# Pooled attention and two feed-forward blocks on one core: the sums of v and the first w1/w2 conversions placed later in the fold

## The chip, the core and the metric

The kernel runs on one core of a Trainium2 chip. The core has TensorE (PE in the profile: matrix products and transposes, results in PSUM), VectorE (DVE), ScalarE (ACT), GpSimd (POOL) and SyncE (SP); the last two mainly issue DMA transfers here. Each engine works off its own instruction queue; engines wait for one another through semaphores. The metric is the device time of one execution in microseconds (us).

## What is computed

The reference, cut to its core:

```python
k_p = k.reshape(B, H, Sp, 8, D).mean(axis=3)      # B=8, H=8, S=576, D=64, Sp=72
v_p = v.reshape(B, H, Sp, 8, D).mean(axis=3)
attn = softmax(q @ k_p.T / sqrt(D))
x = (attn @ v_p).transpose(0, 2, 1, 3).reshape(4608, 512)
x = ((x @ w1) * (x @ w2)) @ w3 @ w_out            # 512 -> 1024 -> 1024 -> 512
xn = x / rms(x) * rms_g
out = (silu(xn @ w_gate) * (xn @ w_val)) @ w_out2 # 512 -> 1536 -> 512
```

## The kernel before

**The fold.** The product of w3 and w_out does not depend on the tokens, so the kernel computes it first (loop `for n in range(NW3)`, 16 tiles of w3). Weights arrive as 64-bit words of which a conversion makes float32. For each w3 tile that takes, in this order: a load on SP (L127), L144 and L147 on ScalarE, L165 and L174 on VectorE, and L177 on VectorE, which writes the tile `f`. TensorE transposes `f` (`tr_w3`, L576) into a PSUM tile, ScalarE copies that out as `hl` (L578), and TensorE makes four products with it (L681), summing in four PSUM banks `wps`. After eight tiles the sums are split into a high and a low part (L100 on ScalarE, L101 on VectorE: `wph`, `wpl`) and stored to DRAM from POOL (L700, L701).

**The attention of batch 0 and the first conversions of w1 and w2 run inside the fold.** They stand in a list `aux` of small steps, which a `Ticker` deals out after the products from the 31st on. `att_steps.flat()` gives the steps of the attention: for each of five query tiles (128 tokens, the last 64) the scores of four heads at a time (`step_S`: L338 on TensorE, the maximum L350 on VectorE, four exponentials L353 on ScalarE), the transposes of q (`step_Q`, L320, L325), the norm (`step_N`: L364, L365, L366 on VectorE), and the transposes of the tile before (`step_T`: L388, copied out by L393). `step_v` adds up pairs of rows of v (L260, L264 on VectorE; the other halvings were done by an accumulating DMA); `av_steps` then multiplies with v (L441) and writes the attention output as a high and a low part (L448 on ScalarE, L449 on VectorE).

The list `side` holds ten steps: `w_tiles` (which allocates), six steps that convert the first four pieces of w1, and three that begin on w2. A w1 or w2 piece takes L144 on ScalarE, L153, L165, L174 and L177 on VectorE, then a split into a high part (L100) and a low part (L101). `side` is spread evenly over `aux` from place `half` on.

**What sets the order.** The program is written as a sequence of steps, and a scheduling layer turns it into one queue per engine; it may move instructions within limits, except those marked `keep_in_program_order` (L144, L165, the first sum of v L260, and the pinned conversions among them). The order on each engine is fixed when the program is built.

**Buffers that tie loads to steps.** The pool `raw` has three buffers. Through them go, in turn, the two halves of batch 0's k, the left half of its v (`kv_369`), then the four pieces of w2 (`raw_469`, `raw_471`, `raw_473`, `raw_475`), then batch 1's k (`kv_881`, `kv_884`) and the left half of its v (`kv_887`). So `raw_473` is loaded when `kv_369` has been summed, and `kv_884` when `raw_473` has been converted. Each half of k or v is loaded in two transfers: a plain one from SP (L254) and an adding one from POOL (L255) when the first has landed.

After the fold the kernel multiplies the attention output of token block 0 with w1 and w2 (`ab`, lines 104 to 106), and from there attention of the next batch runs between these products. The time after 131 us is that of the token blocks and of the second feed-forward block.

Of the kernel before, what the change touches and what calls it, by code (L numbers as in the profile page):

```python
# [21 lines left out]
def kernel(  # L22
# [248 lines left out]
    def att_steps(b):  # L271
# [36 lines left out]
        def step_Q(g, hf):  # L308
            if 2 * g >= NTL:
                return  # L310
            tiles = TILES[2 * g : 2 * g + 2]
            nu, n = len(tiles), tiles[0][1]
            qt = q_t[g].rearrange("s u h d -> s u (h d)")
            if hf == 0:
                qT_t[g] = at_p.tile([P, 2, NP, P], F32, tag="qT", name="qT", bufs=2)
            qT = qT_t[g]
            if hf < nu:
                ps = apsum()
                for p in range(NP):
                    nc.tensor.transpose(  # L320
                        ps[:, p * P : p * P + n],
                        qt[:n, hf, p * P : (p + 1) * P],
                        ident[:n, :n],
                    )
                nc.scalar.copy(  # L325
                    qT[:, hf, :, :n], ps.rearrange("d (p s) -> d p s", p=NP)[:, :, :n]
                )
            if hf == 1:
                q_t.pop(g)
                load_q(g + 2)  # L330

        def step_S(t, hf):
            s0, n = TILES[t]
            ps = apsum()
            if hf == 0:
                s_t[t] = sbuf[t % len(sbuf)]
            for p in (2 * hf, 2 * hf + 1):
                nc.tensor.matmul(  # L338
                    ps[:n, (p % 2) * 2 * SP : (p % 2 + 1) * 2 * SP],
                    qT_t[t // 2][:, t % 2, p, :n],  # L340
                    kT[:, p, :],
                    start=True,
                    stop=True,
                )
            pv = ps[:n, : 4 * SP].rearrange("t (h s) -> t h s", s=SP)
            if hf == 0:
                mx_t[t] = at_p.tile([P, H, 1], F32, tag="mx", name="mx", bufs=2)
                den_t[t] = at_p.tile([P, H, 1], F32, tag="den", name="den", bufs=2)
            mx = mx_t[t][:n, 4 * hf : 4 * hf + 4, :]
            nc.vector.tensor_reduce(out=mx, in_=pv, axis=AX.X, op=ALU.max, negate=True)  # L350
            for j in range(4):
                h = 4 * hf + j
                nc.scalar.activation(  # L353
                    s_t[t][:n, h, :SP],
                    pv[:, j, :],
                    AF.Exp,
                    bias=mx[:, j, :],
                    accum_out=den_t[t][:n, h, :],
                )

        def step_N(t):
            s0, n = TILES[t]
            den = den_t.pop(t)
            nc.vector.tensor_scalar_add(den[:n], den[:n], 1e-9)  # L364
            nc.vector.reciprocal(out=den[:n], in_=den[:n])  # L365
            nc.vector.tensor_tensor(  # L366
                out=s_t[t][:n, :, :SP],
                in0=s_t[t][:n, :, :SP],
                in1=den[:n].to_broadcast([n, H, SP]),
                op=ALU.mult,  # L370
            )

        def step_T(t, hf):
            s0, n = TILES[t]
            if t == 0 and hf == 0:
                st8["aT", b] = at_p.tile([SPP, H, S], F32, tag="aT", name="aT")
            aT = st8["aT", b]
            if b >= 2:
                for i in range(2 * hf, min(2 * hf + 2, n // 32)):
                    for kb in range(SPP // 32):  # L380
                        nc.vector.transpose(  # L381
                            aT[32 * kb : 32 * kb + 32, :, s0 + 32 * i : s0 + 32 * i + 32],
                            s_t[t][32 * i : 32 * i + 32, :, 32 * kb : 32 * kb + 32],
                        )
                return
            ps = apsum()
            for j in range(4):
                nc.tensor.transpose(  # L388
                    ps[:SP, j * P : j * P + n], s_t[t][:n, 4 * hf + j, :SP], ident[:n, :n]
                )  # L390
            src = ps[:SP].rearrange("s (h t) -> s h t", h=4)[:, :, :n]
            dst = aT[:SP, 4 * hf : 4 * hf + 4, s0 : s0 + n]
            nc.scalar.copy(dst, src)  # L393
# [11 lines left out]
        def flat():  # L405
            steps = [step_kT, lambda: step_Q(0, 0), lambda: step_Q(0, 1)]
            for t in range(NTL):

                def d(t=t):
                    if t > 0:  # L410
                        step_T(t - 1, 0)
                    step_N(t)

                def e(t=t):
                    if t > 0:
                        step_T(t - 1, 1)

                steps += [
                    lambda t=t: step_S(t, 0),
                    lambda t=t: step_Q(t // 2 + 1, t % 2),  # L420
                    lambda t=t: step_S(t, 1),
                    d,
                    e,
                ]
            steps[20:20] = [step_v]
            return steps

        return SimpleNamespace(
            flat=flat, k0=step_k0, k1=step_k1, q=load_q, kT=step_kT, Q=step_Q,
            S=step_S, N=step_N, T=step_T, load_v=load_v, v=step_v,  # L430
        )
# [26 lines left out]
    def av_steps(b, i):  # L458
        return [lambda p=p: av_step(b, i, p) for p in range(NP)]
# [191 lines left out]
    aux[8:8] = [s0(*js[4:])]  # L651
    aux += [s0(*j1), lambda: A.T(NTL - 1, 0), lambda: A.T(NTL - 1, 1)]
    aux += av_steps(0, 0)
    half = 11
    side = [w_tiles] + c0[0] + c0[1][:3]
    for n, st in enumerate(side):
        aux.insert(half + (len(aux) - half) * n // len(side), st)
# [273 lines left out]
    half = [pos[2 * n] + pos[2 * n + 1] for n in range(KF1)]  # L931
# [649 lines left out]
```

## Time and profile before

| what | value |
|---|---|
| three runs | 1597.33, 1599.2, 1599.76 us (median 1599.2) |
| the profiled execution | 1597.47 us |
| its span, first to last instruction | 1595.4 us |
| TensorE busy | 1575.3 us (99%) |
| VectorE busy | 1101.3 us (69%) |
| ScalarE busy | 722.3 us (45%) |

A row of the timeline gives the start in us from the span's start, the length, engine, line, operation, written tile <- read tiles, shapes and count; in brackets how long the engine had been idle before, and what ended that. Lengths of neighbours overlap: what an operation costs in a full queue is the distance from its start to the next. A product of two float32 matrices is two or more instructions in the trace, so a row "x4" of L681 is two products. Busy times of TensorE are modelled, so a busy TensorE can still be slower than it might be.

### The profile page before, as it was taken

How to read it: one execution, taken by the hardware profiler on the slowest of the kernel's cores; microseconds unless marked ns; L12 is line 12 of the kernel's file. 1: busy time of each engine (PE TensorE's matmuls, PEld its weight loads, DVE VectorE, ACT ScalarE, POOL GpSimd, SP SyncE). 2: the span in 40 equal slices, each digit the busy share in tenths (PEclk: the TensorE clock that was granted, in tenths of full speed). 3: DMA queues.
4: the chain of work that ended last, by engine and by line, in shares of the span. 5: the costliest groups of instructions: out<-in, count | busy, mean ns of one | idle time of the engine just before them, and what ended most of it. 6: DMA issues, size and time to landing. Idle time of an engine off the chain costs nothing.

```text
span 1595.4 us, 22251 instructions
## 1 busy us (share of the span) xinstructions
PE 1575.3 (99%) x8114; PEld 1297.4 (81%) x8114; DVE 1101.3 (69%) x1945; ACT 722.3 (45%) x1692; POOL 81.4 (5%) x70
## 2 busy tenths in 40 slices
PE   7999999999999999999999999999999999999999
PEld 3567877877877888888888898898898899899888
DVE  7787789978985357789443447686469647775556
ACT  6867444444442245576422434344424433534422
POOL 0011100110000000014000000000000000000000
PEclk9999999999999999999999999999999999999999
DMA  9986644654461268888977666687666866676663
GB/s 281 314 247 128 149 140 125 160 131 132 108 241 47 93 260 325 315 321 298 322 244 244 211 188 195 196 256 227 192 198 200 286 188 191 198 241 185 190 187 97
DMA packets 197262, 328.96 MB, mean 206 GB/s; under 512 B 53657, under 2 KB 100761, under 8 KB 191522
## 3 DMA queue, kind: packets, MB, share of 16 engines
q1 hardware_dynamic: 182338, 305.48, 60.1%
q0 software_dynamic: 14816, 22.07, 6.2%
q8 instruction: 64, 1.05, 0.3%
q14 instruction: 44, 0.36, 0.1%
HBM read 250.89 MB, written 76.58 MB: 205 GB/s over the span
## 4 chain that ended last, share of the span: by engine, by line
PE 85%; DVE 9%; DMA 3%; ACT 1%; issue 1%; SPq 0%; DVEq 0%; POOLq 0%
PE ps L104 20%; PE ps L106 20%; PE ps L105 20%; PE y L106 4%; PE y L105 4%; PE y L104 4%; DVE aT L381 4%; PE o L104 2%; PE o L105 2%; PE o L106 2%; DMA raws<-in_moe_w_out_dram 2%; PE pa L441 2%; PE pa L338 2%; DMA kv<-in_k_dram 1%; PE wps L681 1%
## 5 line engine op out<-in xcount | busy, mean ns | idle before, releaser
L104 PE MATMUL ps<-xf,wr 128*128 128x512 f32 x576 | 225.1, 394 | 0.1
L105 PE MATMUL ps<-xf,wr 128*128 128x512 f32 x576 | 224.5, 390 | 0.0
L106 PE MATMUL ps<-xf,wr 128*128 128x512 f32 x576 | 224.4, 390 | 0.0
L1144 DVE TENSOR_TENSOR f<-y,f 128x512 f32<-128x512 f32 x48 | 33.1, 689 | 167.9 <-PE y L106 157.1
L381 DVE STREAM_TRANSPOSE aT<-s 32x256 f32<-32x256 f32 x324 | 140.8, 435 | 5.2
L1264 ACT COPY f<-ps 128x512 f32<-128x512 f32 x144 | 84.3, 586 | 128.3 <-PE ps L106 127.1
L104 PEld LDWEIGHTS ps<-xf,wr 128*128 128x128 f32 x576 | 108.1, 188 | 27.0 <-DVE f L1144 5.3
L106 PEld LDWEIGHTS ps<-xf,wr 128*128 128x128 f32 x576 | 108.1, 188 | 22.9
L105 PEld LDWEIGHTS ps<-xf,wr 128*128 128x128 f32 x576 | 108.2, 188 | 21.1
L353 ACT ACTIVATE s<-pa,mx 128x72 f32<-128x72 f32 (+1 forms) x280 | 85.6, 337 | 81.5 <-DVE mx L350 81.4
L104 PE MATMUL ps<-xh,w1h 128*128 128x512 f32 x288 | 117.6, 408 | 0.0
L106 PE MATMUL ps<-xh,w1l 128*128 128x512 f32 x288 | 112.8, 392 | 0.0
L105 PE MATMUL ps<-xl,w1h 128*128 128x512 f32 x288 | 112.8, 392 | 0.0
L104 PE MATMUL ps<-xh,w2h 128*128 128x512 f32 x288 | 112.6, 391 | 0.0
L106 PE MATMUL ps<-xh,w2l 128*128 128x512 f32 x288 | 112.3, 390 | 0.0
L105 PE MATMUL ps<-xl,w2h 128*128 128x512 f32 x288 | 112.2, 390 | 0.0
L590 ACT COPY f<-ps 128x512 f32<-128x512 f32 x70 | 41.6, 602 | 77.0 <-PE ps L106 73.2
L1144 DVE TENSOR_TENSOR f<-ps,f 128x512 f32<-128x512 f32 x96 | 65.0, 687 | 15.4 <-ACT hh L1274 8.2
L1144 DVE TENSOR_TENSOR acc<-ps,acc 128x512 f32<-128x512 f32 (+1 forms) x80 | 49.0, 633 | 33.8 <-PE ps L106 33.5
L104 PEld LDWEIGHTS ps<-xh,w1h 128*128 128x128 f32 x288 | 54.1, 188 | 17.4 <-issue 4.2
L105 PE MATMUL ps<-o,hf 128*128 128x256 f32 x240 | 67.9, 283 | 0.0
L106 PE MATMUL ps<-o,hf 128*128 128x256 f32 x240 | 67.9, 283 | 0.0
(250 smaller groups left out, 3917.5 us busy)
## 6 DMA issues: line engine op xcount, KB each, us to landing
wr<-wd SPq DMA_DIRECT2D x168, 512.0 KB
o<-od SPq DMA_DIRECT2D x96, 512.0 KB
hr<-hd SPq DMA_DIRECT2D x32, 512.0 KB
wd<-wst SPq DMA_DIRECT2D x16, 1024.0 KB
od<-ost SPq DMA_DIRECT2D x12, 1024.0 KB
wr<-wd SPq DMA_DIRECT2D x48, 256.0 KB
hd<-hh SPq DMA_DIRECT2D x33, 256.0 KB
q<-in_q_dram SPq DMA_DIRECT2D x32, 256.0 KB
```

The costliest lines, as they stand in the source:

```text
L104: nc.tensor.matmul(o, lh, rh, start=first, stop=False, skip_group_check=part)
L105: nc.tensor.matmul(o, lh, rl, start=False, stop=False, skip_group_check=part)
L106: nc.tensor.matmul(o, ll, rh, start=False, stop=last, skip_group_check=part)
L338: nc.tensor.matmul(ps[:n, (p % 2) * 2 * SP : (p % 2 + 1) * 2 * SP], qT_t[t // 2][:, t % 2, p, :n], kT[:, p, :], start=True, stop=True,)
L353: nc.scalar.activation(s_t[t][:n, h, :SP], pv[:, j, :], AF.Exp, bias=mx[:, j, :], accum_out=den_t[t][:n, h, :],)
L381: nc.vector.transpose(aT[32 * kb : 32 * kb + 32, :, s0 + 32 * i : s0 + 32 * i + 32], s_t[t][32 * i : 32 * i + 32, :, 32 * kb : 32 * kb + 32],)
L441: nc.tensor.matmul(ps[j * D : (j + 1) * D, :n], st8["vp", b][:, h * D : (h + 1) * D], st8["aT", b][:SP, h, c0 : c0 + n], start=True, stop= ...
L590: nc.scalar.copy(a0[i, m], ps)
L681: nc.tensor.matmul(wps[i], wt[:, i * P : (i + 1) * P], wo[j // 4][:, j % 4, :], start=j == 0, stop=j == KF1 - 1,)
L1144: nc.vector.tensor_tensor(out=out, in0=in0, in1=in1, op=op)
L1264: nc.scalar.copy(t, bank)
```

## The change

Two numbers: `step_v`, the sums of v, is put at place 27 of `flat()` instead of 20, which is behind the scores and the norm of the last query tile; and `half`, from where the ten steps of `side` are spread over `aux`, is 15 instead of 11. Nothing is added or removed.

```diff
-            steps[20:20] = [step_v]
+            steps[27:27] = [step_v]
...
-    half = 11
+    half = 15
     side = [w_tiles] + c0[0] + c0[1][:3]
     for n, st in enumerate(side):
         aux.insert(half + (len(aux) - half) * n // len(side), st)
```

VectorE, from the norm of the third query tile (L366, tile `s0_120`) to the L177 of the w3 tile that TensorE transposes next. Before (`f_581` is the w3 tile, the others are w1 pieces):

```order
L366 TENSOR_TENSOR s0_120<-s0_120,den_567 128x8x72
L153 TENSOR_SCALAR f_622<-raws_134 128x512
L165 SCALAR_TENSOR_TENSOR raws_137<-raws_137 128x512
L101 TENSOR_TENSOR w1l_503<-f_550,w1h_502 128x512
L177 ISA f_588<-raws_137,f_588 128x1024
L350 TENSOR_REDUCE mx_640<-ps_637 128x4
L165 SCALAR_TENSOR_TENSOR raws_134<-raws_134 128x512
L174 TENSOR_SCALAR f_622<-f_622 128x512
L177 ISA f_581<-raws_134,f_581 128x1024
```

After, the last twelve rows of that stretch (`f_583` is the w3 tile); between the norm and them stand six more, L153, L165, L153, L177, L165 and L174:

```order
L350 TENSOR_REDUCE mx_632<-ps_629 128x4
L177 ISA f_590<-raws_136,f_590 128x1024
L101 TENSOR_TENSOR w1l_542<-f_564,w1h_541 128x512
L153 TENSOR_SCALAR f_639<-raws_134 128x512
L165 SCALAR_TENSOR_TENSOR raws_137<-raws_137 128x512
L174 TENSOR_SCALAR f_613<-f_613 128x512
L101 TENSOR_TENSOR w1l_542<-f_590,w1h_541 128x512
L177 ISA f_613<-raws_137,f_613 128x1024
L165 SCALAR_TENSOR_TENSOR raws_134<-raws_134 128x512
L174 TENSOR_SCALAR f_583<-f_583 128x512
L174 TENSOR_SCALAR f_639<-f_639 128x512
L177 ISA f_583<-raws_134,f_583 128x1024
```

The w3 conversion stood eighth behind the norm and now stands eighteenth, with the w1 conversions (L101: their last step) ahead of it.

VectorE, the sums of v (L260, L264). Before, from the fourth w1 piece's L177 to the w3 tile `f_647`, which stands two rows further on:

```order
L177 ISA f_622<-raws_134,f_622 128x1024
L260 TENSOR_TENSOR kv_369<-kv_369 72x4x128
L350 TENSOR_REDUCE mx_640<-ps_673 128x4
L264 TENSOR_TENSOR vp_667<-kv_369 72x256
L260 TENSOR_TENSOR kv_372<-kv_372 72x4x128
L101 TENSOR_TENSOR w1l_503<-f_622,w1h_502 128x512
L264 TENSOR_TENSOR vp_667<-kv_372 72x256
L364 TENSOR_SCALAR den_641<-den_641 128x8
L174 TENSOR_SCALAR f_647<-f_647 128x512
L365 RECIPROCAL den_641<-den_641 128x8
L174 TENSOR_SCALAR f_693<-f_693 128x512
L366 TENSOR_TENSOR s1_121<-s1_121,den_641 128x8x72
```

After, from the norm of the last query tile on (`f_702` is the last w3 tile, `raw_469` and `raw_471` are pieces of w2):

```order
L366 TENSOR_TENSOR s0_120<-s0_120,den_696 64x8x72
L153 TENSOR_SCALAR f_738<-raw_469 128x512
L165 SCALAR_TENSOR_TENSOR raws_135<-raws_135 128x512
L174 TENSOR_SCALAR f_738<-f_738 128x512
L177 ISA f_702<-raws_135,f_702 128x1024
L260 TENSOR_TENSOR kv_369<-kv_369 72x4x128
L264 TENSOR_TENSOR vp_745<-kv_369 72x256
L260 TENSOR_TENSOR kv_372<-kv_372 72x4x128
L264 TENSOR_TENSOR vp_745<-kv_372 72x256
L153 TENSOR_SCALAR f_764<-raw_471 128x512
L165 SCALAR_TENSOR_TENSOR raw_469<-raw_469 128x512
L174 TENSOR_SCALAR f_764<-f_764 128x512
```

The sums moved from ahead of the last two w3 tiles to behind the last of them.

SP, from batch 1's right half of v on. Before:

```order
L254 DMA kv_890<-in_v_dram 72x4x256
L127 DMA raw_475<-in_moe_w2_dram 128x1024
L254 DMA kv_881<-in_k_dram 72x4x256
L127 DMA rawp_1048<-in_moe_w2_dram 128x1024 x2
L127 DMA rawp_1051<-in_moe_w2_dram 128x1024 x2
L254 DMA kv_884<-in_k_dram 72x4x256
L254 DMA kv_887<-in_v_dram 72x4x256
L127 DMA rawp_1531<-in_moe2_w_gate_dram 128x1024 x2
```

After:

```order
L254 DMA kv_890<-in_v_dram 72x4x256
L127 DMA raw_475<-in_moe_w2_dram 128x1024
L127 DMA rawp_1048<-in_moe_w2_dram 128x1024
L254 DMA kv_881<-in_k_dram 72x4x256
L127 DMA rawp_1048<-in_moe_w2_dram 128x1024
L127 DMA rawp_1051<-in_moe_w2_dram 128x1024 x2
L127 DMA rawp_1531<-in_moe2_w_gate_dram 128x1024
L254 DMA kv_884<-in_k_dram 72x4x256
L254 DMA kv_887<-in_v_dram 72x4x256
L601 DMA hd0_95<-hh_911 128x512
```

One load of w_gate (`rawp_1531`, whose buffer held `wph`) moved ahead of the loads of `kv_884` and `kv_887`, and one load of w2 ahead of that of `kv_881`. On POOL the store of the second `wph` and `wpl` (L700, L701) moved ahead of the adding transfer of `kv_881`.

## Rows read from the trace of the kernel before

**Rows 1.** Busy time by stretch: length, busy by engine, clock, DMA share, GB/s

```profile
57.00:99.00 42.00, 38.49 (x170) 20.42 (x171) 36.64 (x77) 34.76 (x112) 5.79 (x7) 1.00 0.89 250
...
86.00:87.00 1.00, 1.00 (x10) 0.97 (x9) 1.00 (x3) 1.00 (x6) 0.00 (x0) 1.00 0.00 0
...
131.00:1595.40 1464.40, 1459.37 (x7643) 1228.91 (x7641) 1000.24 (x1745) 631.89 (x1469) 65.98 (x49) 1.00 0.64 201
```

**Rows 2.** Waits of TensorE, 0 to 131 us: total, times, longest

```profile
PE ps L576 <- DVE f L177: 10.8, 5, 6.9
...
PE pa L301 <- DVE kv L264: 0.5, 1, 0.5
```

**Rows 3.** Timeline of TensorE, fold: start, length, operation, idle before

```profile
69.16 1.02 PE L681 MATMUL wps<-wo,hl 128*128 128x512 f32 x2
70.03 0.60 PE L388 MATMUL ps<-ident,s 128*72 128x128 f32 x4
70.46 0.66 PE L338 MATMUL ps<-kT,qT 128*128 128x144 f32 x4
...
75.74 0.63 PE L576 MATMUL ps<-ident,f 128*128 128x128 f32 x4 [1.19 <-DVE f L177]
...
83.38 0.63 PE L576 MATMUL ps<-ident,f 128*128 128x128 f32 x4 [2.00 <-DVE f L177]
...
87.76 0.60 PE L576 MATMUL ps<-ident,f 128*128 128x128 f32 x4
...
98.49 0.50 PE L104 MATMUL ps<-xh,w1h 128*128 128x512 f32 x1
```

**Rows 4.** Timeline of VectorE, third query tile's norm to next w3 conversion

```profile
70.79 0.76 DVE L366 TENSOR_TENSOR s<-s,den 128x576 f32<-128x576 f32 x1
71.47 0.42 DVE L153 TENSOR_SCALAR f<-raws 128x512 f32<-128x512 f32 x1
71.80 0.69 DVE L165 SCALAR_TENSOR_TENSOR raws<-raws 128x512 int32<-128x512 int32 x1
72.41 0.68 DVE L101 TENSOR_TENSOR w1l<-f,w1h 128x512 fp32r<-128x512 f32 x1
73.01 0.68 DVE L177 CUSTOM_DVE_ANT_0 f<-raws,f 128x1024 uint16<-128x1024 uint16 x1
73.61 0.45 DVE L350 TENSOR_REDUCE mx<-ps 128x4 f32<-128x288 f32 x1
73.98 0.68 DVE L165 SCALAR_TENSOR_TENSOR raws<-raws 128x512 int32<-128x512 int32 x1
74.58 0.42 DVE L174 TENSOR_SCALAR f<-f 128x512 int32<-128x512 int32 x1
74.91 0.68 DVE L177 CUSTOM_DVE_ANT_0 f<-raws,f 128x1024 uint16<-128x1024 uint16 x1
```

**Rows 5.** Timelines of ScalarE and VectorE, second query tile's last exponentials, L364

```profile
60.92 0.33 ACT L353 ACTIVATE s<-ps,mx 128x72 f32<-128x72 f32 x1
...
62.28 0.17 DVE L364 TENSOR_SCALAR den<-den 128x8 f32<-128x8 f32 x1 [0.90 <-ACT s L353]
```

**Rows 6.** Timelines of POOL, SP and VectorE, batch 1's k and what precedes it

```profile
98.74 1.23 POOL L700 DMA_DIRECT2D wpd<-wph  x1
...
101.78 0.33 SPq L254 DMA_DIRECT2D kv<-in_k_dram  x1
...
110.72 0.85 SPq L127 DMA_DIRECT2D rawp<-in_moe_w_gate_dram  x2
...
112.87 1.25 POOL L255 DMA_DIRECT2D kv<-in_k_dram  x1 [12.34 <-DVE f L177]
...
122.22 0.69 DVE L260 TENSOR_TENSOR kv<-kv 72x512 f32<-72x512 f32 x1 [1.94 <-DMA kv<-in_k_dram]
```

**Rows 7.** Timeline of TensorE, its first row, and the page's granted clock

```profile
6.90 1.08 PE L576 MATMUL ps<-ident,f 128*128 128x128 f32 x4 [6.90 <-DVE f L177]
...
PEclk9999999999999999999999999999999999999999
```

## Prediction

> **What bounds the kernel now.** I read the busy time by stretch first [rows 1]. From 131 us to the end TensorE is busy 1459.37 of 1464.40 us, and the change reorders nothing there, so whatever it does before 131 us is added to the whole span or taken from it, one to one. The change acts from about 58 us, in the fold. Between 57 and 99 us TensorE is busy 38.49 of 42.00 us: 3.5 us of idle time is all that an order of the fold can win. The waits of TensorE [rows 2] name it: the transposes of a w3 tile (L576) wait for VectorE's last conversion step (L177), five times, 6.9 us of it at the very start. In the timeline [rows 3] the large ones are 1.19 us at 75.74 and 2.00 us at 83.38. So the fold alternates: TensorE works off one w3 tile (transposes, four products L681, pieces of attention), and VectorE has to have the next tile converted by then. VectorE runs its queue strictly in the written order [rows 4]: what stands ahead of an L177 delays it. That makes the question simple: what stands ahead of each of the w3 L177s now?
>
> **The change, part by part.** No instruction is added or removed; all that moves are the sums of v, ten pieces of w1/w2 work, and what the scheduler makes of it.
>
> Prices, from row start to next row start: L153 and L174 0.33, L165, L177 and L101 0.60, L350 0.37, L366 0.68 [rows 4]; transposes of one tile 0.43, one product L681 0.87, two score products L338 0.5 in the queue and 0.66 until the result stands [rows 3]; from the first exponential of a half tile to L364 1.36 us (60.92 to 62.28) [rows 5]; from the start of an L177 to the L576 that waits for it 0.83 (74.91 to 75.74) [rows 3, 4].
>
> (a) Early on, the w1 conversions no longer stand between the halves of the second query tile. Its second exponentials follow the first at once, 0.58 us earlier than 60.92, L364 comes at 61.7, the norm ends at 62.8. The w3 conversion that stood ahead of the norm now stands behind it: L177 at 63.5, L576 at 64.4. TensorE has four products to do meanwhile and waits about 1 us there. From there: scores of the third tile from 64.8 and 65.7, exponentials from 66.1 and (one conversion on ScalarE in between) 67.8, L364 at 69.2, L366 from 69.6 to 70.3, where before it started at 70.79 [rows 4]. So far a gain on VectorE of 1.2 us.
>
> (b) The bunch. Before, seven operations stand between that L366 and the next w3 L177 (4.1 us, 70.79 to 74.91). Now seventeen do, because the four w1 conversions start later and come in one row: seven at 0.33, nine at 0.60, one at 0.37, together 8.1 us. L177 starts at 78.4 and L576 at 79.3, where before it was 75.74. TensorE has the same work behind it there and would be ready at 75.3 (0.75 us behind 75.74 less 1.19, from its wait in (a)). It waits 4.0 us instead of 1.19.
>
> (c) After that each w3 tile hangs on the one before, through all engines: L576 and two score products 1.1, the maximum until ScalarE starts 0.5, exponentials 1.36, L364 to L366 with another L350 in between 0.7, L366 0.68, three conversion steps 1.8, L177 to L576 0.83: 7.05 us, so L576 at 86.4. TensorE's work in that time is 5.8 us (transposes of three tiles 1.3, scores 1.05, four products 3.45): a wait of 1.2 us, where before 2.00 stood at 83.38. The next link is 6.75 us (one copy on ScalarE ahead of the exponentials; L153, L165, L174 ahead of the L177): L576 at 93.1, a wait of 1.4 us, where before (87.76) there was none.
>
> (d) The rest. Before, 10.73 us lie between 87.76 and the first product with w1 (98.49) [rows 3]. Of these, two products (1.8 with their change-over) are already done at that point now, and two more change-overs between products and attention cost 0.2: 9.1 us, so 102.2. **The fold ends 3.7 us later.** The sums of v themselves cost nothing new: they end at 93.9 (left group) and 94.8, just as TensorE comes to the first product with v (94.1), covered by the last tile's transposes; if they came later, each us would count fully.
>
> (e) The transfers that hang on moved steps. The third piece of w2 can be loaded only when the left sums of v are done (same buffer), so at 94 and no longer far ahead. Behind its conversion step L153 and its ScalarE step L144 stand VectorE's and ScalarE's work on the attention output, which the products at 102.2 need 2.8 us later on these queues. A load of up to 5.4 us is therefore hidden. The trace bounds such a load from below by 0.5 MB at the stretch's 250 GB/s (2.1 us [rows 1]), from above by the 11 us from 101.78 to the POOL issue at 112.87 that waits for it among others [rows 6], with four loads queued ahead. At 86 us the DMA engines stand idle [rows 1], as they will when this load is alone; I take 4 us, near the lower end: no cost.
>
> (f) Batch 1's k. TensorE's next wait is for its second half (0.5 us, pa L301 [rows 2]), which lands at 122.22 [rows 6]. SP asked for it at 101.78, then for w_gate at 110.72, which had waited for the store of the folded weights (POOL, 98.74): 12 us. Now SP asks for w_gate first, so k waits behind the store. The store starts with the fold's end, at 101.5, and has fewer loads beside it: done between 109 and 113.5, I take 111. Then 4.5 us for the first half, as little else is queued, and the 9.35 us that the second took (112.87 to 122.22): 124.9. TensorE wants it 3.7 us after its own old readiness, at 125.4. So it is just in time, and the old 0.5 us wait disappears. Bounds: 121 (store at 109, both halves quicker), and 134 (store at 113.5, first half 11 us).
>
> **Sum:** +3.7 -0.5 = +3.2 us. The profiled execution took 1597.47 us (span 1595.4, 2.1 around it); 1600.7 on that footing. The median of the three runs shown is 1599.2, 1.7 above it, so I forecast 1602.4. What a measurement of this kernel can tell from no change is about 0.2%, 3.2 us: my sum lies right on that edge.
>
> **Rivals.** *Batch 1's k comes late.* For: the new order of SP, and a chain of three waits. Against: less traffic at that time. If the store is done only at 113.5, k is there at 127.4, 5.2 us later than before, and that takes the place of 3.2: 1604.4; with a slow first half up to 1608. It decides from 125.4 on.
>
> *The clock falls.* The first products after the idle 6.90 us at the start run at half speed: 1.08 us for four transposes [rows 7] against 0.63 after the 2.00 us wait [rows 3], though the row of granted clock shows the full level (2.4 GHz) in every slice [rows 7]. The wait of 4.0 us in (b) lies between the two. Two tiles' transposes and two products at half speed would add about 2.6 us: 1605.0. The Trainium skill (TensorE: Matmul & The Clock Gate, section HAM oscillation — how this bites in real kernels) says that a long enough idle gap sends TensorE back to half rate until it has been kept busy again; the start of this trace agrees with it, its 2.00 us wait shows no fall.
>
> *Third piece of w2 late.* From a load of 5.4 us on, up to 5.6 more: about 1606.
>
> *Lag paid back.* TensorE's recorded ends are modelled, and waits in (c) may be shorter than my sum if ScalarE or VectorE gain on their queues; a lag under 2 us gives 1599 to 1601.
>
> *Faster.* The sums of v (L260, L264) stood ahead of the L177 behind the 2.00 us wait; with them gone that wait could vanish, and with the norms no longer behind w1 work the 1.19 as well: -3.2 us, 1596.0. It decides at one point: the L177 of (b) would have to start by 74.5, so the seventeen operations would have to take 4.2 us instead of 8.1. Nothing in the rows makes VectorE that fast.
>
> **How the numbers follow.** Forecast (2 to 4.5 us more) 0.50, half of it within 0.2%; k late 0.22; clock 0.10; w2 late 0.03; lag paid back 0.10; faster 0.05. Slower by over 0.2%: 0.25 + 0.22 + 0.10 + 0.03 = 0.60; within: 0.25 + 0.10 = 0.35; faster 0.05. The range goes from 1599.5 (most of the paid-back case left out below) to 1607.5 (the worst of k and clock left out above).
>
> **What would show it.** In the new profile: one long wait of TensorE for an L177 near 75 us, about 4 us, then two of 1.2 to 1.4 us, and the first product with w1 near 102. If the waits for L177 after 57 us sum to less than 3.5 us, (b) is wrong. If the clock fell, the transposes after the long wait take 1.08 instead of 0.63. If k is late, pa L301 waits for more than 0.5 us. If the fold ends at 102 and the time is still unchanged, the premise that nothing after it gives time back is wrong.

## Result, and the profile after

The changed kernel takes 1608.9 us (median of six runs, 1606.03 to 1610.13) against 1597.41 us for the kernel before (six runs): ratio 1.0069, interval 1.0058 to 1.0079, so 11 us slower. The forecast was 1602.4 us, the range ended at 1607.5. The sign was right, but the forecast held under a third of the size. Part of its closeness is luck: it stood on a median of 1599.2 us from three runs, 1.8 us above the median of all six. The profiled execution took 1609.25 us, its span 1607.4 us: 12.0 us more than before.

Busy time by stretch of the changed kernel, columns as in [rows 1]. The third number from the end of each row is the granted clock:

```profile
78.00:80.00 2.00, 1.11 (x5) 1.14 (x6) 1.68 (x4) 0.00 (x0) 0.00 (x0) 0.50 1.18 244
80.00:82.00 2.00, 2.00 (x10) 1.77 (x10) 0.46 (x1) 1.12 (x5) 0.00 (x0) 0.50 0.73 250
...
132.00:134.00 2.00, 1.15 (x7) 1.16 (x8) 2.00 (x5) 0.00 (x0) 0.00 (x0) 0.65 0.39 129
134.00:136.00 2.00, 2.00 (x11) 1.46 (x11) 1.97 (x5) 1.60 (x4) 0.00 (x0) 0.50 0.70 190
```

The waits of TensorE over the whole span; the second had been 0.5 [rows 2]:

```profile
PE ps L576 <- DVE f L177: 13.1, 5, 6.6
PE pa L301 <- DVE kv L264: 2.9, 1, 2.9
```

The timeline of TensorE, which answers to [rows 3]:

```profile
56.37 0.63 PE L576 MATMUL ps<-ident,f 128*128 128x128 f32 x4 [0.48 <-DVE f L177]
...
78.89 1.09 PE L576 MATMUL ps<-ident,f 128*128 128x128 f32 x4 [3.89 <-DVE f L177]
...
94.64 0.63 PE L576 MATMUL ps<-ident,f 128*128 128x128 f32 x4 [1.18 <-DVE f L177]
...
104.68 0.50 PE L104 MATMUL ps<-xh,w1h 128*128 128x512 f32 x1
...
129.63 0.29 PE L301 MATMUL pa<-ident,kv 72*128 72x72 f32 x2
132.85 0.50 PE L301 MATMUL pa<-ident,kv 72*128 72x72 f32 x2 [2.93 <-DVE kv L264]
...
135.40 0.80 PE L104 MATMUL ps<-xh,w1h 128*128 128x512 f32 x1
...
207.86 1.20 PE L338 MATMUL pa<-kT,qT 128*64 128x144 f32 x8
```

Two things stand here that the kernel before does not have: a wait of 3.89 us in the fold and one of 2.93 us at batch 1's k; and behind each of them a granted clock of 0.50, which is the level of 1.2 GHz. The four transposes at 78.89 take 1.09 us instead of 0.63, the product at 135.40 takes 0.80 instead of 0.50.

**Where the 12.0 us come from.** The first loads take differently long from execution to execution (the transposes at 56.37 started between 56.1 and 59.7 in the profiles of this study), so I measure the fold from these transposes to the first product with w1: 98.49 - 57.08 = 41.4 us before, 104.68 - 56.37 = 48.3 us after, **+6.9**, from a start 0.7 earlier. From there to the first L301 it is 24.64 us before and 24.95 after, +0.3. The wait at pa L301: 2.93 against 0.48, +2.45. Between this L301 and the last scores of that batch lie 196.05 - 123.90 = 72.15 us before and 207.86 - 132.85 = 75.01 after: **+2.9**, behind the second fall of the clock. Together 11.8, and 0.2 in the long rest. TensorE's timeline of the kernel before, the three rows used:

```profile
123.13 0.29 PE L301 MATMUL pa<-ident,kv 72*128 72x72 f32 x2
123.90 0.34 PE L301 MATMUL pa<-ident,kv 72*128 72x72 f32 x2 [0.48 <-DVE kv L264]
...
196.05 1.19 PE L338 MATMUL pa<-kT,qT 128*64 128x144 f32 x8
```

### The profile page after: what moved, and what is told of

Same layout as the page of the kernel before. It is cut to its first block, busy times and chain, and to the rows that moved or that the text cites. A ratio compares the mean times of both kernels' runs of the same rounds, so it can differ in the third digit from the quotient of the medians.

```text
span 1607.4 us, 22252 instructions
## 1 busy us (share of the span) xinstructions
PE 1582.1 (98%) x8114; PEld 1301.2 (81%) x8114; DVE 1102.1 (69%) x1945; ACT 722.8 (45%) x1692; POOL 80.4 (5%) x70
## 4 chain that ended last, share of the span: by engine, by line
PE 87%; DVE 7%; DMA 2%; ACT 1%; SPq 1%; issue 1%; DVEq 0%; ACTq 0%
PE ps L104 21%; PE ps L106 20%; PE ps L105 20%; PE y L104 4%; PE y L106 4%; PE y L105 4%; DVE aT L381 3%; PE o L105 2%; PE o L104 2%; PE o L106 2%; PE pa L338 2%; PE pa L441 2%; SPq L127 1%; DMA raws<-in_moe_w_dram 1%; ACT s L353 1%; PE pa L320 1%
```

## Experiments

Theory after the result: (1) the bunch of w1 conversions makes the wait of 3.89 us, as forecast; (2) the sums of v move batch 1's k behind the load of w_gate on SP, and so behind the store of the folded weights; (3) both waits let the clock fall, which costs again. The main rivals: one edit is behind everything; the late k is only a consequence of the late fold; the clock falls for a reason of its own.

The table is the yardstick for all runs. "Fold" is the length as above, "k" the wait at pa L301, "half clock" the stretches below full clock behind 57 us and ahead of the last products, all from the profiled execution; the ratio is to runs of the kernel before on the same chip.

| kernel | fold us | k us | half clock us | ratio, interval |
|---|---|---|---|---|
| before | 41.4 | 0.48 | none | 1 |
| changed | 48.3 | 2.93 | 6.8 and 6.8 | 1.0069 (1.0058 to 1.0079) |
| v_only | 40.3 | 3.08 | 6.8 | 1.0023 (1.0012 to 1.0033) |
| side_only | 45.1 | none | 3.4 | 1.0021 (1.0010 to 1.0031) |
| k_first | 48.4 | none | 6.8 | 1.0048 (1.0033 to 1.0063) |
| k_first_fill | 46.4 | 0.17 | none | 1.0025 (1.0016 to 1.0033) |
| k_fill | 48.9 | filled | 3.4 and 3.4 | 1.0048 (1.0034 to 1.0062) |
| both_fill | 46.5 | filled | none | 1.0042 (1.0029 to 1.0056) |
| late_tr | 50.0 | 0.25 | 3.4 and 6.8 | 1.0064 (1.0049 to 1.0079) |
| late_tr_fill | 45.3 | 4.00 | 3.4 | 1.0055 (1.0042 to 1.0067) |
| late_fill_k | 45.2 | 0.73 | none | 1.0019 (1.0010 to 1.0028) |
| v_k_first | 40.4 | none | none | 0.9989 (0.9981 to 0.9998) |
| v_k_pair | 39.6 | none | none | 0.9985 (0.9976 to 0.9994) |
| before_fill | 41.4 | none | none | 0.9993 (0.9985 to 1.0002) |

### One edit at a time: v_only and side_only

```diff
 v_only (against the changed kernel)
-    half = 15
+    half = 11
 side_only (against the changed kernel)
-            steps[27:27] = [step_v]
+            steps[20:20] = [step_v]
```

> Only the sums of v are moved (place 27); the w1 pieces are dealt out from place 11, as before the change. Theory (each edit has its own cost: the w1 pieces that now stand in a row ahead of a w3 conversion cost the fold, the sums of v cost batch 1's k its place in SP's queue): no wait for an L177 above 2.5 us after 57 us, full clock between 70 and 90 us, the first product with w1 at 97 to 99.5 us; but SP asks for the load of w_gate ahead of k's second half, which waits for the store of the folded weights, so pa L301 waits about 2.9 us and the clock falls behind it (about 3.4 us more): 1602 to 1604 us. Rival (the late k is only a consequence of the late fold): no wait for k above 0.5 us, 1596 to 1598 us. Rival (the sums of v make the long wait themselves): a wait near 4 us and 1606 us or more.

> Only the w1 and w2 pieces are dealt out from place 15; the sums of v stay at place 20, as before the change. Theory (each edit has its own cost): the w3 conversion again stands some 17 operations behind the third query tile's norm, so TensorE waits 3 to 4.5 us for it, and if the wait is the one of the changed kernel the clock falls behind it; the first product with w1 at 102 to 105 us. SP asks for k ahead of w_gate as in the kernel before, so pa L301 waits for k under 1 us and the clock stays up there: 1601 to 1604 us. Rival (a late fold is what makes k late): pa L301 waits over 2 us and the time is 1607 us or more. Rival (the sums of v make the long wait): no wait above 2 us in the fold, 1597 to 1599 us.

TensorE in v_only:

```profile
57.28 0.63 PE L576 MATMUL ps<-ident,f 128*128 128x128 f32 x4 [0.48 <-DVE f L177]
...
75.94 0.63 PE L576 MATMUL ps<-ident,f 128*128 128x128 f32 x4 [1.26 <-DVE f L177]
...
97.62 0.50 PE L104 MATMUL ps<-xh,w1h 128*128 128x512 f32 x1
...
125.93 0.50 PE L301 MATMUL pa<-ident,kv 72*128 72x72 f32 x2 [3.08 <-DVE kv L264]
```

TensorE in side_only, and its busy time by stretch (clock third from the end):

```profile
79.89 0.63 PE L576 MATMUL ps<-ident,f 128*128 128x128 f32 x4 [3.86 <-DVE f L177]
...
87.20 0.63 PE L576 MATMUL ps<-ident,f 128*128 128x128 f32 x4 [0.20 <-DVE f L177]
...
102.31 0.50 PE L104 MATMUL ps<-xh,w1h 128*128 128x512 f32 x1
```

```profile
78.00:80.00 2.00, 0.11 (x1) 0.14 (x2) 2.00 (x5) 0.53 (x1) 0.00 (x0) 1.00 1.04 275
80.00:82.00 2.00, 2.00 (x14) 1.81 (x15) 2.00 (x5) 0.60 (x2) 0.00 (x0) 0.70 1.12 271
82.00:84.00 2.00, 2.00 (x6) 1.21 (x5) 1.97 (x5) 1.61 (x8) 0.00 (x0) 0.50 0.89 289
```

The two edits have one harm each, as the theory says. The dealing out of the w1 pieces alone makes the long wait (3.86 us); the sums of v alone make the fold 1.1 us shorter, not longer, and make k late (3.08 us) although the fold is early: the late k is no consequence of a late fold. v_only's ten runs lie between 1597.17 and 1603.63 us, their median 1599.96 is below the 1602 to 1604 expected; the profiled one (1602.29) is one with a late k and a fallen clock. The mean granted clock of every run is on record: it is 0.998 in the four runs of v_only that took 1602.29 to 1603.63 us, and 0.999 or 1.000 in the six that took 1597.17 to 1600.21. So these six lost less to the clock; whether they also had k earlier can't be read, since only one run has a trace. side_only's median, 1600.32, is 0.7 us below the 1601 to 1604 expected. The two ratios add up to 1.0044, the change has 1.0069: together the edits cost 4 us more than one by one. Part of that is in the fold: in side_only the last w3 tile, the second behind the long wait, is not waited for, where the changed kernel waits 1.18 us, at full clock in both. So the last wait of (c) in the prediction needs both edits; the rest of the 4 us was not traced.

In side_only the same wait as in the changed kernel leaves the clock at full level until it ends; it falls 0.9 us after TensorE has taken up work, and for half as long. So a wait of 3.9 us does not fix what the clock does.

### The late k: k_first and k_fill

```diff
 k_first (against the changed kernel)
-        nc.sync.dma_start(out=r, in_=w[:, :, :n])
+        (tc.keep_in_program_order if b == 1 and src is k else (lambda z: z))(nc.sync.dma_start(out=r, in_=w[:, :, :n]))
...
+            cs[z].on_act = True; cs[z].pl = (G, s, kp) == (0, 0, 0)
```

(L127 keeps a load that is marked by `pl` in program order too, so that the one of w_gate stays behind those of k.)

> The changed kernel, but SP's load of k's second half (and of v's left half) for batch 1 is held ahead of the load of w_gate, as in the kernel before; TensorE's queue is the same row for row. Theory (k is late because SP waits with it for the store of the folded weights): the load is asked for at 110 instead of 116.81, pa L301 waits under 0.5 us instead of 2.93, the clock stays at full level between 131 and 140 us, the first product with w1 stays at about 104.7: 5.5 to 6.3 us less, 1602.5 to 1604 us. Rival (k is late through the DMA traffic and POOL's order, not through SP): pa L301 still waits over 2 us, 1607 us or more. Rival (the clock falls at that place whatever TensorE waits): only the wait goes, 2.5 us less, about 1606 us.

SP, POOL and VectorE in the changed kernel, the store and what waits for it, which answers to [rows 6]:

```profile
104.66 0.56 POOL L700 DMA_DIRECT2D wpd<-wph  x1 [1.44 <-ACT wph L100]
...
116.39 0.33 SPq L127 DMA_DIRECT2D rawp<-in_moe_w_gate_dram  x1
116.81 0.85 SPq L254 DMA_DIRECT2D kv<-in_k_dram  x1
...
125.23 1.19 POOL L255 DMA_DIRECT2D kv<-in_k_dram  x1 [15.70 <-DMA kv<-in_v_dram]
...
130.83 0.69 DVE L260 TENSOR_TENSOR kv<-kv 72x512 f32<-72x512 f32 x1 [4.25 <-DMA kv<-in_k_dram]
```

The same load in k_first, and TensorE there:

```profile
110.58 0.33 SPq L254 DMA_DIRECT2D kv<-in_k_dram  x1
```

```profile
79.80 1.09 PE L576 MATMUL ps<-ident,f 128*128 128x128 f32 x4 [3.86 <-DVE f L177]
...
105.44 0.50 PE L104 MATMUL ps<-xh,w1h 128*128 128x512 f32 x1
...
130.36 0.63 PE L301 MATMUL pa<-ident,kv 72*128 72x72 f32 x4
```

As expected: 1603.56 us, k asked for at 110.58 instead of 116.81, no wait, no fall of the clock behind it; the w3 tile, its wait and the fall in the fold stay. The place of one load in SP's queue was worth 5.3 us by the medians and 5.1 by the spans (1607.4 to 1602.3), 3.4 by the ratios (1.0069 to 1.0048), which go back to other runs of the kernel before.

k_fill separates wait and clock there. It leaves the order alone and puts work that nobody reads into the wait (22 transposes of a constant ahead of the late ones, inserted into the finished queue so that no other row moves):

```diff
+    prog[at:at] = [
+        x.__replace__(name=f"I-{910000 + n}", ins=(x.ins[0], data), sync_info=None) for n in range(22)
+    ]
```

> The changed kernel with 22 more transposes of a constant, some 2.7 us of TensorE work that nobody reads, directly ahead of the transposes of batch 1's second half of k; every other row is as in the changed kernel. Theory (the late k costs twice: TensorE's wait of 2.93 us, and some 3.4 us by the half clock behind it): the wait shrinks to under 0.5 us, its place is taken by the added work, the clock stays at 1.00 from 131 to 140 us, and 2.5 to 3.5 us are won: 1605 to 1606.5 us. Rival (the clock has nothing to do with that wait): 1608 us or more.

TensorE in k_fill:

```profile
133.68 1.56 PE L301 MATMUL pa<-ident 72*128 72x72 f32 x22
135.07 0.33 PE L301 MATMUL pa<-ident,kv 72*128 72x72 f32 x2
```

The clock stays up behind it and the ratio falls to 1.0048. But in its profiled execution k came early, and the clock fell once more in the fold, at 98.8 us, where the wait ahead of it (1.18 us at 96.93) is one that the changed kernel had without a fall. Its median (1607.57, five runs) is a little above the 1605 to 1606.5 expected. So k_fill alone is weak; both_fill (below) settles the clock's share.

### The clock in the fold: k_first_fill and both_fill

```diff
+    prog[tr[0] : tr[0]] = [
+        x.__replace__(name=f"I-{900000 + n}", ins=(x.ins[0], x.ins[0]), sync_info=None if n else free)
+        for n in range(32)
+    ]
```

> The kernel of k_first with 32 more transposes of a constant matrix, 3.4 us of TensorE work that nobody reads, put into TensorE's queue directly ahead of the four transposes that waited 3.86 us for VectorE; every other row of every queue is as in k_first. Theory (the half clock comes from TensorE standing idle): the transposes of the w3 tile start at 79.8 as before, the granted clock stays at 1.00 from 75 to 90 us, they take 0.63 instead of 1.09, and the first product with w1 comes 1.8 to 2.6 us earlier than 105.44: 1601 to 1602 us, though TensorE does 3.4 us more. Rival (the added work costs its time, or the clock falls whatever stands in the gap): 1603.5 to 1607 us.

TensorE in k_first_fill, and its clock:

```profile
75.68 3.66 PE L576 MATMUL ps<-ident 128*128 128x128 f32 x32
79.71 0.63 PE L576 MATMUL ps<-ident,f 128*128 128x128 f32 x4 [0.38 <-DVE f L177]
...
103.57 0.50 PE L104 MATMUL ps<-xh,w1h 128*128 128x512 f32 x1
```

```profile
78.00:80.00 2.00, 1.62 (x16) 1.41 (x15) 2.00 (x5) 0.34 (x1) 0.00 (x0) 1.00 1.11 297
80.00:82.00 2.00, 2.00 (x19) 1.80 (x17) 0.96 (x3) 1.22 (x6) 0.00 (x0) 1.00 0.96 232
```

TensorE does 3.4 us more, and the kernel is faster: ratio 1.0025 instead of 1.0048. The w3 tile comes at the same time (79.71 against 79.80), but the clock is at 1.00 throughout and the fold 2.0 us shorter (46.4 against 48.4). The median, 1602.47, is 0.5 us above the range of the expectation, against runs of the kernel before that were slower there too (1598.89).

both_fill does the same in the three waits of the changed kernel, 32 and 10 ahead of the w3 tiles that waited 3.89 and 1.18 us, 36 smaller ones ahead of k:

```diff
+    for n, count in ((13, 32), (15, 10)):
...
+        x.__replace__(name=f"I-{910000 + n}", ins=(x.ins[0], data), sync_info=None) for n in range(36)
```

> The changed kernel, row for row, with transposes of a constant that nobody reads in its three long waits: 32 ahead of the w3 tile that waited 3.89 us, 10 ahead of the one that waited 1.18, 36 small ones ahead of the second half of batch 1's k (2.93 us). Theory (the two half clock stretches make up 1.9 and 3.4 of its 11 to 12 us): the clock is at 1.00 from 20 us on, all waits start and end where they did, 4.5 to 5.5 us are won: 6 to 7.5 us above the kernel before. Rival (the clock accounts for less, the waits for more): 9 us or more above it.

In its profile the clock is at 1.00 from 9 us to the end of the products, its median is 1604.35 against 1598.17 us, ratio 1.0042: 6.2 us above the kernel before instead of 11. So the two stretches at half clock make up 4 to 5 us of the 11, and the waits and the order 6 to 7. TensorE in both_fill:

```profile
130.21 0.34 PE L301 MATMUL pa<-ident,kv 72*128 72x72 f32 x2
...
202.33 1.19 PE L338 MATMUL pa<-kT,qT 128*64 128x144 f32 x8
```

From the late transposes to the last scores of that batch it takes 72.12 us, as the kernel before does (72.15), where the changed kernel takes 75.01. So the 2.9 us behind k are the clock's.

### Filling the wait with work of the kernel: late_tr, late_tr_fill, late_fill_k

```diff
-            if i == 1 and n + 1 < NW3:
+            if i == (1, 3)[n == 12] and n + 1 < NW3:
```

> The changed kernel, but the transposes of the fourteenth w3 tile (the one TensorE waits 3.89 us for at 78.89) are given out two products later in the program, so that scores, transposes of attention weights and two products, some 2.8 us of TensorE work, stand ahead of the wait instead of behind it. VectorE's queue up to that L177 is nearly the same. Theory (the wait is VectorE's queue, and its length is what makes the clock fall): L576 again at 78.5 to 79.5, but the wait in front of it is 1 to 1.5 us, the granted clock stays at 1.00 from 70 to 90 us, four transposes take 0.63 instead of 1.09, and the first product with w1 comes 2.5 to 5 us earlier than 104.68; the late k and the clock behind it stay: 1603.5 to 1606.5 us. Rival (the clock falls for another reason than the wait, as the load of the array before it): the clock falls all the same and the time is 1607 us or more.

This expectation failed. The wait became shorter, but only by 0.9 us (2.98), the fold longer (50.0 us), and the time is that of the changed kernel. TensorE in late_tr, and its clock:

```profile
79.94 0.63 PE L576 MATMUL ps<-ident,f 128*128 128x128 f32 x4 [2.98 <-DVE f L177]
...
94.16 0.63 PE L576 MATMUL ps<-ident,f 128*128 128x128 f32 x4 [1.74 <-DVE f L177]
```

```profile
96.00:98.00 2.00, 2.00 (x3) 0.50 (x2) 2.00 (x5) 0.56 (x3) 0.00 (x0) 0.50 0.78 231
```

The clock fell behind a wait of 2.98 us and again behind one of only 1.74. So "a shorter wait keeps the clock" is no rule here. late_tr_fill puts transposes of a constant into both waits:

```diff
+    for n, count in ((13, 24), (15, 14)):
```

> The kernel of late_tr with transposes of a constant that nobody reads ahead of the two late w3 tiles: 24 (2.6 us) where TensorE waited 2.98 us, 14 (1.5 us) where it waited 1.74. All else is the same row for row. Theory (late_tr lost what it won to two stretches at half clock, of 3.3 and 6.5 us): the clock stays at 1.00 from 70 to 105 us, and the first product with w1 comes 45 to 46 us behind the transposes near 57 us instead of 50.0: 3.5 to 5 us less than late_tr, 5 to 7 us above the kernel before. Rival (the order itself is slower): distance 48 or more, 8 us or more above the kernel before.

The fold is 45.3 us, as expected, with the clock up, and 1.1 us shorter than in k_first_fill (46.4); but the time hardly moved (1.0055, 8.8 us above the kernel before, where 5 to 7 were expected). The gain went into a wait of 4.00 us at k, and into 3.4 us at half clock behind it; TensorE in late_tr_fill:

```profile
128.03 0.29 PE L301 MATMUL pa<-ident,kv 72*128 72x72 f32 x2
132.32 0.34 PE L301 MATMUL pa<-ident,kv 72*128 72x72 f32 x2 [4.00 <-DVE kv L264]
```

late_fill_k is late_tr_fill with the three lines of k_first.

> The kernel of late_tr_fill with SP's load of k's second half held ahead of the load of w_gate, as in k_first; TensorE's queue is the same row for row. late_tr_fill brought the fold 4.8 us forward against late_tr, and its time stayed the same, with a wait of 4.00 us at pa L301 where late_tr had 0.25. Theory (the gain was given back at k, which waits for the store of the folded weights, and that store was done only 1.2 us earlier though it began 3.3 us earlier): with k asked for ahead, pa L301 waits under 0.5 us, the clock stays at 1.00 behind it, and the gain stays: the first product with w1 45.3 us behind the transposes near 57 us, 3 to 4.5 us above the kernel before (ratio 1.002 to 1.003). Rival (k is late for another reason, or the gain is lost elsewhere): 7 us or more above it (ratio 1.0045 or more).

With k asked for ahead of w_gate the gain stays: 1601.18 us, ratio 1.0019, 3.0 us above the kernel before by the ratio. Wait at k 0.73 us, a little more than expected. So three things stood one behind the other, and to take one away showed only once the next was gone.

### What is good in the change: v_k_first and v_k_pair

v_k_first is k_first with the w1 pieces dealt out as before: only the sums of v move, and k keeps its place on SP.

```diff
-    half = 15
+    half = 11
```

> Only the sums of v are moved (place 27, w1 pieces from place 11), and SP's load of k's second half is held ahead of the load of w_gate. Theory (moving the sums of v alone shortens the fold by 0.9 us, and only SP's order spoils it): the first product with w1 at 97.3 to 97.9, pa L301 waits under 0.3 us, no half clock after 20 us: 1595 to 1596.2 us, below the kernel before by 0.5 to 1.7 us. Rival (holding k ahead of w_gate costs as much elsewhere, or the clock falls at another wait): 1596.7 us or more.

It is faster than the kernel before: ratio 0.9989 (0.9981 to 0.9998), 1597.15 against 1598.89 us. The median misses the 1595 to 1596.2 us expected, beside runs of the kernel before that took 2.2 us more than those beside v_only (1596.69 us).

The fold's end in v_k_first shows why the sums of v do not bring more. TensorE, the products with v (L441):

```profile
89.97 1.07 PE L441 MATMUL ps<-aT,vp 72*64 72x512 f32 x2
90.97 1.98 PE L681 MATMUL wps<-wo,hl 128*128 128x512 f32 x4
92.89 1.93 PE L441 MATMUL ps<-aT,vp 72*64 72x512 f32 x6
```

There are eight such products, two for each PSUM tile, one for each half of its partitions. In the kernel before they stand in rows of four, two and two; here, and in the changed kernel, the scheduling layer took the first from its partner. v_k_pair moves it back (one instruction, two places further, behind two products L681).

```diff
+    av = [x for x in prog if type(x).__name__ == "InstMatmult" and "'vp_" in str(x.ins)][:2]
+    at = [next(i for i, z in enumerate(prog) if z.name == x.name) for x in av]
+    prog.insert(at[1] - 1, prog.pop(at[0]))
```

> The kernel of v_k_first, but the first two products of the attention weights with v (L441, two heads that use the left and the right half of TensorE's columns) stand next to each other again, as the other three pairs do: the first is moved behind the two products L681 that had come between. Theory (two such products side by side take 0.93 us together, and each takes as much alone, so that the separation costs one time 0.93 us): the four products of the first two pairs stand in one row of 1.9 us, the first product with w1 comes 0.9 us earlier as counted from the transposes near 57 to 59 us (39.4 us instead of 40.37), and the time is 0.7 to 1.1 us below v_k_first's. Rival (the longer rows were a matter of the record, each product costs 0.47 wherever it stands): the distance stays at 40.4 and the time is the same.

TensorE in v_k_pair:

```profile
90.55 1.94 PE L441 MATMUL ps<-aT,vp 72*64 72x512 f32 x8
```

Four products now take 1.9 us, where one alone took 1.00 (89.97 to 90.97) and the three others 1.86 (92.89 to 94.75): a pair takes as long as a single one. The fold becomes 0.8 us shorter (39.6). The time, 1595.97 against 1598.17 us, ratio 0.9985 (0.9976 to 0.9994), is the best of all kernels here, 2.4 us below the kernel before by the ratio, 1.9 by the spans of the two profiled executions (1593.5 and 1595.4). Against v_k_first the intervals overlap, so that the 0.8 us rests on the trace, not on the times.

### The kernel before, with its own waits filled

before_fill puts 10 and 16 transposes of a constant ahead of the w3 tiles that waited 1.19 and 2.00 us [rows 3].

```diff
+    for n, count in ((13, 10), (14, 16)):
```

> The kernel before, with transposes of a constant that nobody reads in two waits of TensorE: 10 ahead of the w3 tile that waited 1.19 us, 16 ahead of the one that waited 2.00. Theory (waits of 1 to 2 us let the clock fall in some executions only; the runs of the kernel before show mean clocks from 0.998 to 1.000): mean clock 0.999 or more in every run, a median 0.3 to 1.2 us lower. Rival (the kernel before never loses to its clock, or the added work pushes the fold back): same or up to 1 us higher.

Ratio 0.9993 (0.9985 to 1.0002): not to be told from no change. The mean clock was 1.000 in nine of its eleven runs, and in eleven of 21 of the kernel before beside it. That alone shows little, since the clock also falls at the very end of a run: v_k_first's profiled execution has a mean of 0.999, and its only fall behind 20 us is there (0.84 over the last 5.8 us, 0.9 us lost). A mean of 0.998 is too low for that, as it means 2.4 us lost or more. Five of the 74 recorded runs of the kernel before have it, and they took 1598.5 to 1601.59 us. So there the clock fell earlier as well, but at which wait no trace shows.

## Why the prediction was wrong

Against the sum of 3.2 us, three steps failed: (d), 0.9 us too short; (f), which took 0.5 us off at k where 2.45 were added; and the clock, which the sum put at nothing and which cost 1.9 us in the fold and 2.9 behind k.

**What bounds the kernel, and that the fold's shift is paid one to one: right.** Every us that the fold or the wait at k gained or lost stood in the time, until the next wait took it: from the last scores of batch 1 (207.86 us in the changed kernel) to the end, all fourteen profiled executions take 1399.3 to 1399.8 us.

**(a), (b), (c): right.** The w3 tile that matters came 22.5 us behind the transposes near 57 us (forecast 79.3 - 57.08 = 22.2), with a wait of 3.89 (forecast 4.0). VectorE worked through the norm's last step and the seventeen operations in 8.95 us, 69.11 to 78.06 (forecast 8.8, from the prices of [rows 4]):

```profile
69.11 0.76 DVE L366 TENSOR_TENSOR s<-s,den 128x576 f32<-128x576 f32 x1
...
78.06 0.68 DVE L177 CUSTOM_DVE_ANT_0 f<-raws,f 128x1024 uint16<-128x1024 uint16 x1
```

Where the clock was held up (k_first_fill), the two tiles behind it came after 6.95 and 6.88 us (forecast 7.05, though the rounded terms add up to 6.97, and 6.75). The waits there were 0.69 and 1.18 us (forecast 1.2 and 1.4); in the changed kernel, with TensorE at half clock, the first of them was gone.

**(d) was 0.9 us too short.** From the last tile to the first product with w1 I took 9.1 us, it was 10.0. I priced the products with v by their number; their order split a pair that otherwise takes the time of one product. v_k_first and v_k_pair show it: 10.0 and 9.2 us for that leg. TensorE's queue in the changed kernel has the same split, one product and then three instead of four in a row, and I priced them alike:

```profile
95.77 1.07 PE L441 MATMUL ps<-aT,vp 72*64 72x512 f32 x2
...
98.69 1.93 PE L441 MATMUL ps<-aT,vp 72*64 72x512 f32 x6
```

In the changed kernel itself the pair was not put back; its leg is as long as v_k_first's.

**(e): right.** SP asked for w2's third piece at 95.58 us, and VectorE's conversion waited 0.67 us for it:

```profile
99.91 0.43 DVE L153 TENSOR_SCALAR f<-raw 128x512 f32<-128x512 f32 x1 [0.67 <-DMA raw<-in_moe_w_dram]
```

So the load took at most 4.3 us (forecast 4), and TensorE waited for nothing there.

**(f) was the first large error, and it is one of sizes.** The mechanism was as written: SP holds k behind the load of w_gate, which waits for the store. But the store took 11.7 us, from its issue on POOL to the load that waits for it (104.66 to 116.39), where I took 9.5; the first half of k took 8.4 (116.81 to 125.23), where I took 4.5; the second 5.6 (125.23 to 130.83), where I took 9.35. Together 26 us instead of 23.4, so that with the forecast end of the fold, too, k would have come 2.3 us behind the 125.4 at which it decides. The sum also let the store begin at 101.5, 0.7 us ahead of the fold's end by (d), and names no row for that: it began 0.25 us behind the fold's end in the kernel before [rows 3, 6], and 0.02 ahead of it in the changed one. From 102.4 on, (f)'s own terms give 125.8, already late. The expectation that a transfer is quicker when less is queued has no row to rest on: in v_only, late_tr, late_tr_fill, k_fill and both_fill the store took 12.1, 9.4, 11.6, 9.5 and 9.9 us, and when it began 3.3 us earlier (late_tr to late_tr_fill) it was done only 1.2 us earlier. What sets its length stays open.

**The clock was the second error, the largest, and one of method.** The rival was priced well (2.6 us at half clock; measured 1.9 to 2.0 in the fold by k_first_fill, 2.9 behind k). Its chance of 0.10 was too low: between the wait of 2.00 us that had done no harm and the 6.90 of the start there was no row at all, and I leaned on the nearer end. Above all I treated the two rivals as exclusive. They are not: a late k is itself a wait of about 3 us, and can bring a fall of the clock of its own. All together, 5.0 (order) + 1.9 (clock in the fold) + 0.3 (up to k) + 2.45 (k) + 2.9 (clock behind k) + 0.2 (the rest) - 0.7 (start) = 12.0 us, where the upper end of the range held one rival at a time. The Trainium skill (TensorE: Matmul & The Clock Gate, section HAM oscillation — how this bites in real kernels), which the prediction named, says that a long enough idle gap sends TensorE back to half rate; both long waits of the changed kernel agree with it, while the other runs show that the length of a wait alone does not tell (below).

## What to carry to other kernels

A wait of TensorE that a change makes can cost more than its length: ask what the clock may do behind it, and add that to the upper end of the forecast, for each such wait, rather than hold it as a case by itself. When pieces of work are dealt out later, count what then stands in a row ahead of the one conversion that the bottleneck waits for; and follow each queue past the change, since here one load that was asked for behind another was worth 3.4 to 5.3 of the 11 us. Rivals that can come true together have to be added before the end of a range is set.

## What the runs showed of the hardware that I had not expected

The granted clock does not follow the length of a wait alone. Waits of 3.89 and 3.86 us brought 6.8 us at 0.50 in the changed kernel and in k_first, beginning while TensorE still stood; the same wait in side_only brought 3.4 us, beginning 0.9 us after work had been taken up; 2.98 and 1.74 us in late_tr brought 3.4 and 6.8 us; a wait of 1.18 us stood ahead of 3.4 us in k_fill and of none in the changed kernel; 2.00 us in the profiled execution of the kernel before brought none. Executions of one kernel differ in it, and with it in time by several us: in the changed kernel 1606.03 us at a mean clock of 0.999, 1607.53 at 0.998, and 1608.55 to 1610.13 at 0.996 and 0.997. In side_only the mean does not sort the times (1599.61 us at 0.997, 1600.82 at 0.999).

TensorE work that nobody reads can save time: 3.4 us of transposes in a wait made the fold 2.0 us shorter (k_first to k_first_fill), and the clock stayed at 1.00.

Two products that write the two halves of a PSUM tile's partitions take 0.93 us together (two such pairs took 1.87, 90.55 to 92.42 in v_k_pair) and 0.93 to 1.00 each when other products stand between them. The Trainium skill (TensorE: Matmul & The Clock Gate, section Part 3: Packing small matmuls — row/col tiling) says that products placed on different parts of the array run at the same time; the rows of v_k_first and v_k_pair agree.
